# Attention followed by hash-routed experts: a new instruction order in attention, a small slot table for two experts, and the full routing moved behind expert 0

## The chip, the core and the metric

The kernel runs on one core of one Trainium2 chip. A core has TensorE (PE, matrix products), VectorE (DVE) and ScalarE (ACT) for elementwise work, GpSimd (POOL), which also issues the casting and indirect transfers, and SyncE (SP), which issues plain ones. Each engine takes its own instructions in order. The metric is device time in microseconds (us), the median over runs: 375.97 us before the change (3 runs, 375.48 to 377.52).

## The reference

Attention with normed queries and keys over 8 batches, 12 heads, 448 tokens and head size 64; its output, as 3584 rows of 768, goes to one of 8 experts each, chosen by a hash of the token's id.

```python
def rmsnorm(x, g):
    rms = np.sqrt(np.mean(x * x, axis=-1, keepdims=True) + 1e-06)
    return x / rms * g
q_n, k_n = (rmsnorm(q, g_q), rmsnorm(k, g_k))
scores = 1.0 / np.sqrt(64) * np.matmul(q_n, k_n.transpose(0, 1, 3, 2))
scores = scores - np.max(scores, axis=-1, keepdims=True)
attn = np.exp(scores)
attn = attn / (np.sum(attn, axis=-1, keepdims=True) + 1e-09)
x = np.matmul(attn, v)                      # -> (3584, 768)
...
expert_idx = token_ids * np.int64(2654435761) % np.int64(8)
for e in range(8):
    mask = expert_idx == e
    h = np.maximum(x[mask] @ w1[e], 0.0)    # w1[e]: 768 x 1024
    out[mask] = h @ w2[e]                   # w2[e]: 1024 x 768
```

## The kernel before

Attention goes over 48 steps, one for a pair of heads of a batch (6 a batch), in groups of three. For each group, q and k are squared, summed with TensorE, and normed; for each step they are transposed into one PSUM bank (`ps_qk`, one buffer), copied out, multiplied to scores (`ps_sc`, three buffers), put through the exponential on ScalarE, and multiplied with v. The result x goes to a scratch in device memory, batch by batch.

```python
def prep_sq(gi, a, on_act=False):            # a: 1 for k, 0 for q
    ...
    if on_act:
        nc.scalar.activation(dst, f, AF.Square, bias=0.0, scale=1.0)
    else:
        nc.vector.tensor_tensor(out=dst, in0=f, in1=f, op=ALU.mult)
...
def transposes(s, evac=True):
    T32 = ps_qk.tile([P, 512], FP32, name="qkT_ps")
    ...  # 4 transposes of k, 4 of q; then transposed(s): kT and qT copied by VectorE
def score(s, j):
    sc = ps_sc.tile([P, 2, 512], FP32, name="sc_ps")
    ...  # j < 3: two matmuls, then
    nc.scalar.activation(expT[:, 2 * j:2 * j + 2, :], sc[:, :, :S], AF.Exp, bias=0.0, scale=1.0)
    ...  # j == 3: one matmul and one half-size exponential
def av_part(s, part):                        # products with v; part 2 ends with
    nc.vector.reciprocal(srec[:], av[:, :, D])
    nc.vector.tensor_tensor(out=x_sb[...], in0=av[:, :, :D], in1=srec[...], op=ALU.mult)
    if hp == HP - 1:
        store_x(b)
```

The order of one step is written out in a loop, with the routing in small pieces (`side`) between the steps, and the loads of weights at fixed steps:

```python
for s in range(1, NS):
    score(s, 1); score(s, 2)
    if nxt: transposes(s + 1)
    score(s, 3)
    if s == NS - 1:
        for kt in range(KT - 1):             # first rows of expert 0
            put_xT(xg_e[kt], xT_e, kt, bank[:].bitcast(FP16)[:, 0:DIN])
    av_part(s - 1, 0); av_part(s - 1, 1)
    if nxt: score(s + 1, 0)
    ...                                      # pre[s], mid[s], av_part(s - 1, 2), post[s]
    if side and s >= 14:
        side.pop(0)()                        # p1 ... p11, 14 pairs of table(c), table_mm
    if s == NS - 4:
        for kt in range(KT - 1):
            gather(xg_e[kt], gidx[:, kt:kt + 1], N_EARLY)
    if hp == 3:
        if b == 3: w_tiles[0] = [load_w1(0, new_w1(w_pool))]
        if b == 4: w_tiles[0].append(load_w2(0, new_w2(w_pool)))
        if b == 5: w_tiles[1] = [load_w1(1, new_w1(w_pool))]
        if b == 6: w_tiles[1].append(load_w2(1, new_w2(w_pool)))
    if b == 6 and hp == 5:
        w_tiles[2] = w_views(); load_w1(2, w_tiles[2][0])
    if b == 7 and hp == 0:
        load_w2(2, w_tiles[2][1])
```

The routing gives every token a slot: expert times 512 plus its rank there. A matmul over 28 columns of tokens then turns that round into `gidx`, the list of tokens for each slot. Its table lies in one of the two buffers for second-layer weights:

```python
tab = w_pool.tile([P, FO, DIN], FP16, name="w2_sb")[:].rearrange("p a b -> p (a b)")
lo1 = tab[:, 0:NTC * P].rearrange("p (c s) -> p c s", s=P)
hi1 = tab[:, NTC * P:NTC * (P + NHI)].rearrange("p (c s) -> p c s", s=NHI)
...
def table(c):
    V.tensor_scalar(out=lo1[:, c], in0=iota_h[:], scalar1=hl[:, 1, c:c + 1], scalar2=None,
                    op0=ALU.is_equal)
    G.tensor_scalar(out=hi1[:, c], in0=iota_h[:, 0:NHI], scalar1=hl[:, 0, c:c + 1],
                    scalar2=tv[:, c:c + 1], op0=ALU.is_equal, op1=ALU.mult)
```

The experts: rows of x are gathered by token, transposed in TensorE through one PSUM buffer (`turn`), multiplied with w1 (`gemm1`, ReLU shared by ScalarE and VectorE), with w2 (`gemm2`), and scattered to the output.

```python
fetch(1, range(KT - 1)); fetch(0, [KT - 1]); fetch(1, [KT - 1]); fetch(2, range(KT))
queue += w_pieces(3)
for e in range(E):
    if e == 0:
        gemm1(w1_sb, xTs[e], h_sb, 0, EARLY)         # EARLY = 384 of up to 480 rows
        overflow_table()
    else:
        if e + 2 < E: fetch(e + 2, range(KT))
        gemm1(w1_sb, xTs.pop(e), h_sb, 0, FIT)
    w_next(2)
    for kt in range(KT):
        if e == 0 and kt == KT - 1:
            turn(0, kt); gemm1(w1_sb, xTs.pop(0), h_sb, EARLY, FIT); turn(1, kt)
        elif e + 1 < E:
            turn(e + 1, kt)
        gemm2(w2_sb, h_sb, kt, gidx[:, c:c + 1])
        w_next(1)
```

Of the kernel before, what the change touches and what calls it, by code (L numbers as in the profile page):

```python
# [19 lines left out]
def kernel(  # L20
# [45 lines left out]

    SL = 7
# [32 lines left out]
    late = consts.tile([P, 1], FP32)  # L100
    tri = consts.tile([P, EH, NTC], BF16)
# [5 lines left out]
    def setup():  # L107
        import dataclasses as _dc
        tid_t32 = _dc.replace(moe_token_ids.tensor, shape=[N * 2], dtype=I32)
        for base in (0, D):  # L110
            nc.sync.dma_start(out=gcol[base:base + D, 0:1], in_=g_q[:, None])
            nc.sync.dma_start(out=gcol[base:base + D, 1:2], in_=g_k[:, None])
        nc.scalar.dma_start(out=tid32[:],
                            in_=bass.AP(tensor=tid_t32, offset=0,
                                        ap=[[2 * NTC, P], [2, NTC], [1, 2]]))

    def setup2():
# [21 lines left out]
        keep_ge(tri[:], [[NTC, EH], [1, NTC]], -1, -1)  # L139
        G.tensor_copy(iota_f[:], iota_i[:])  # L140
# [35 lines left out]
    gidx = rt_keep.tile([P, NHI], I32)  # L176
    ov_i = rt_keep.tile([P, NOV], I32)


    def gather(xg, idx, rows=N):  # L180
        nc.gpsimd.indirect_dma_start(  # L181
            out=xg[:], out_offset=None, in_=x_dram[0:rows, :],
# [24 lines left out]
    with tc.manual_schedule(), \  # L207
# [66 lines left out]
        def prep_sq(gi, a, on_act=False):  # L274
# [5 lines left out]
            if on_act:  # L280
# [4 lines left out]
        def prep_sum(gi, a, wide=False):  # L285
# [3 lines left out]
            if wide:  # L289
# [17 lines left out]


        def prep_rr(gi):
            n = groups[gi][2]  # L310
            ss = st[gi].pop("ss")
            m = 8 * n
            rr = a_st.tile([P, 2, GMAX * 8, 2], FP16, name="rr")
            nc.scalar.activation(ss[:, :, 0:m], ss[:, :, 0:m], AF.Ln, bias=eps_col[:], scale=1.0 / D)
# [3 lines left out]
            st[gi]["n8"] = a_n8.tile([P, 2, GMAX, 4, 2, D], FP16, name="n8")  # L318

        def prep_norm(gi):  # L320
            n = groups[gi][2]
            rr = st[gi].pop("rr")
            n8 = st[gi]["n8"]
            for a in (1, 0):
                f = raw(a, gi).rearrange("p n (hh j) (u t) -> p n hh j u t", hh=2, t=2)
                for hh in range(2):
                    nc.vector.tensor_tensor(
                        out=n8[:, a, 0:n, :, hh, :].rearrange("p n j (u t) -> p n j u t", t=2),
                        in0=f[:, :, hh],
                        in1=rr[:, a, 4 * n * hh:4 * n * hh + 4 * n].rearrange(  # L330
                            "p (n j) t -> p n j t", j=4)[:, :, :, None, :].to_broadcast(
                                [P, n, 4, D // 2, 2]),
                        op=ALU.mult)
# [9 lines left out]

        rt = lambda shape, dt, name: rt_sb.tile(shape, dt, name=name)
        eid = rt([P, NTC], I32, "eid")
        eidf = rt([P, NTC], FP32, "eidf")
        onehot = rt([P, E, NTC], BF16, "onehot")
        oc = rt([P, E], BF16, "oc")
        cmix = rt([P, 2, P], BF16, "cmix")
        et = rt([P, 2, E], FP32, "et")  # L350
        hole = rt([P, E], FP32, "hole")
        offl = rt([P, E], FP32, "offl")
        t1 = rt([P, E], I32, "t1")
        ot = rt([P, E], FP32, "ot")
        ones_e = rt([P, E], FP32, "ones_e")
        add_e = rt([P, E], FP32, "add_e")
        rank = rt([P, E, NTC], FP32, "rank")
        over = rt([P, E, NTC], FP32, "over")
        slot_f = rt([P, NTC], FP32, "slot_f")
        slot_i = rt([P, NTC], I32, "slot_i")  # L360
        parts = rt([P, 2, NTC], I32, "parts")
        hl = rt([P, 2, NTC], FP32, "hl")
        tab = w_pool.tile([P, FO, DIN], FP16, name="w2_sb")[:].rearrange("p a b -> p (a b)")
# [574 lines left out]
```

## Time and profile before

| | |
|---|---|
| time, median of 3 | 375.97 us |
| span of the profiled run | 374.0 us |
| TensorE busy | 341.5 us, 91% of the span |
| VectorE busy | 213.7 us, 57% |
| ScalarE busy | 189.9 us, 51% |
| GpSimd busy | 174.9 us, 47% |
| mean granted TensorE clock | 0.974 of full speed |
| moved by DMA | 64.59 MB, mean 173 GB/s |

Attention takes the first half of the span and the experts the second, and they have different limits, so the shares over the whole span tell little. The prediction reads the profile by stage. A row of a group gives the source line, the engine and operation, what is written and read with shapes, the count, the busy time and the mean in ns of one. A row of waits gives who waited for whom, the total, the number and the longest wait. A row of the timeline gives start, length, and in brackets the idle time ahead of it with what ended it. In the table by stretches, each engine has its busy time and its instruction count; then come the clock, the mean busy share of the DMA engines as the profile gives it, and GB/s. The digits of the forty slices are tenths of a slice's time.

### The profile page before, as it was taken

The page shows a single profiled execution, that of the slowest core. Times are in us where ns is not written, and L with a number is a line of the kernel's source. Part 1 is how long each engine was busy: PE and PEld are TensorE (multiplying, and loading weights), DVE is VectorE, ACT ScalarE, POOL GpSimd, SP SyncE. Part 2 cuts the span into 40 slices and gives each one's busy share as a digit, 9 for nine tenths or more (in the row PEclk, how much of TensorE's full clock was granted, in tenths as well). Part 3 has the DMA queues.
Part 4 walks back from the last instruction along what each step waited for, and adds up shares of the span by engine and source line. Part 5 has one row for each costly group of instructions (what it writes and reads, how often), then busy time and mean ns, then how long its engine had stood idle before and what let it go on. Part 6 is the DMA issues. An engine that isn't in the chain of part 4 may idle for free. (4 is left out here: it accounts for less than half of the span.)

```text
span 374.0 us, 9220 instructions
## 1 busy us (share of the span) xinstructions
PE 341.5 (91%) x3862; PEld 235.2 (63%) x3862; DVE 213.7 (57%) x514; ACT 189.9 (51%) x288; POOL 174.9 (47%) x246
## 2 busy tenths in 40 slices
PE   7778989999989999998199999999999999999992
PEld 3446656666666666765077676766767676666761
DVE  4577989999999999989033332323232323332311
ACT  5776979999989999999202212111211122121110
POOL 8977981027349920300604855555627445302122
PEclk9998999999999999999669999999999999999998
DMA  8999999928999992299804799999999999702113
GB/s 117 163 184 195 190 221 195 221 35 138 193 212 214 226 198 71 30 207 239 231 10 107 147 279 240 253 246 198 257 195 252 228 189 254 256 23 85 58 42 111
DMA packets 53996, 64.59 MB, mean 173 GB/s; under 512 B 22259, under 2 KB 41990, under 8 KB 53568
## 3 DMA queue, kind: packets, MB, share of 16 engines
q0 software_dynamic: 50320, 57.98, 86.8%
q1 hardware_dynamic: 3024, 5.41, 5.1%
q10 hardware_dynamic: 608, 0.59, 0.6%
q8 instruction: 31, 0.51, 0.6%
q14 instruction: 13, 0.11, 0.1%
HBM read 89.68 MB, written 17.30 MB: 286 GB/s over the span
## 5 line engine op out<-in xcount | busy, mean ns | idle before, releaser
L508 ACT ACTIVATE expT<-sc_ps 128x896 bf16<-128x896 f32 x144 | 125.1, 922 | 10.4 <-PE sc_ps L506 9.2
L790 PEld LDWEIGHTS <-h_sb 128*128 128x128 f16 (+1 forms) x512 | 51.2, 104 | 30.5
L790 PE MATMUL o_ps<-w_sb,h_sb 128*128 128x512 f16 (+3 forms) x384 | 65.8, 326 | 0.0
L795 POOL DMA_INDIRECT out_dram<-o_sb,gidx x32 | 32.5, 1017 | 66.2 <-ACT o_sb L794 36.8
L780 ACT ACTIVATE h_sb<-h_ps 128x480 f16<-128x480 f32 (+2 forms) x36 | 18.8, 526 | 85.9 <-PE h_ps L776 81.2
L776 PEld LDWEIGHTS <-w_sb 128*128 128x128 f16 x336 | 44.3, 146 | 16.6 <-issue 2.2
L181 POOL DMA_INDIRECT xg<-x_scratch,gidx x32 | 32.6, 1019 | 46.1 <-DVE x_sb L551 18.4
L782 DVE TENSOR_SCALAR h_sb<-h_ps 128x480 f16<-128x480 f32 (+2 forms) x36 | 21.7, 602 | 54.9 <-PE h_ps L776 52.1
L776 PE MATMUL h_ps<-xT,w_sb 128*128 128x480 f16 x240 | 49.4, 366 | 0.0
L506 PE MATMUL sc_ps<-qT,kT 64*128 64x448 f16 x288 | 44.6, 360 | 3.7 <-DVE qT L497 1.9
L794 ACT COPY o_sb<-o_ps 128x768 f32<-128x768 f32 x16 | 12.8, 800 | 68.0 <-PE o_ps L790 64.6
L530 PEld LDWEIGHTS <-expT 128*128 128x128 bf16 x864 | 37.8, 99 | 9.5 <-DVE x_sb L551 5.7
L530 PE MATMUL av_ps<-v,expT 128*128 128x65 bf16 x864 | 41.1, 195 | 0.7 <-DVE x_sb L551 0.7
L485 PEld LDWEIGHTS <-n 128*128 128x128 f16 x384 | 22.8, 98 | 24.2 <-issue 14.9
L794 DVE COPY o_sb<-o_ps 128x768 f32<-128x768 f32 (+1 forms) x16 | 15.3, 955 | 38.4 <-PE o_ps L790 27.6
L485 PE MATMUL qkT_ps<-ident,n 128*128 128x128 f16 x384 | 30.7, 222 | 5.8 <-DVE ss L306 2.9
L551 DVE TENSOR_TENSOR x_sb<-av_ps,srec 128x448 f16<-128x448 f32 x48 | 29.7, 619 | 1.5
L193 DVE COPY xT<-xT_ps 128x768 f16<-128x768 f16 x28 | 15.4, 552 | 26.1 <-PE xT_ps L192 26.1
L295 PEld LDWEIGHTS <-ident 128*128 128x128 f16 x544 | 23.5, 98 | 9.0 <-issue 6.3
L513 ACT ACTIVATE expT<-sc_ps 128x448 bf16<-128x448 f32 x48 | 26.8, 558 | 1.1 <-PE sc_ps L511 1.1
L495 DVE TENSOR_SCALAR kT<-qkT_ps,g_col 128x512 f16<-128x512 f16 x48 | 23.0, 480 | 4.9 <-PE qkT_ps L485 4.3
L535 PE MATMUL av_ps<-v,expT 128*128 128x130 bf16 x144 | 25.4, 222 | 0.0
(152 smaller groups left out, 476.8 us busy)
## 6 DMA issues: line engine op xcount, KB each, us to landing
w_sb<-in_moe_w_dram POOLq DMA_DIRECT2D x24, 384.0 KB
w_sb<-in_moe_w_dram POOLq DMA_DIRECT2D x8, 768.0 KB
x_scratch<-x_sb SPq DMA_DIRECT2D x15, 288.0 KB, 7.0
w_sb<-in_moe_w_dram POOLq DMA_DIRECT2D x2, 1536.0 KB
qr<-in_moe_w_dram POOLq DMA_DIRECT2D x8, 384.0 KB
kr<-in_k_dram POOLq DMA_DIRECT2D x6, 384.0 KB
qr<-in_q_dram POOLq DMA_DIRECT2D x3, 768.0 KB
vr<-in_v_dram POOLq DMA_DIRECT2D x6, 384.0 KB
```

The costliest lines, as they stand in the source:

```text
L181: nc.gpsimd.indirect_dma_start(out=xg[:], out_offset=None, in_=x_dram[0:rows, :], in_offset=bass.IndirectOffsetOnAxis(ap=idx, axis=0), bou ...
L485: nc.tensor.transpose(T[:, o:o + P], n8[:, a, i, j].rearrange("p h d -> p (h d)"), ident16[:])
L506: nc.tensor.matmul(sc[:, hh, :S], lhsT=kT[64 * hh:64 * hh + 64, P * j:P * j + P], rhs=qT[64 * hh:64 * hh + 64, :], start=True, stop=True)
L508: nc.scalar.activation(expT[:, 2 * j:2 * j + 2, :], sc[:, :, :S], AF.Exp, bias=0.0, scale=1.0)
L513: nc.scalar.activation(expT[:, 6, :], sc[:, 0, :S], AF.Exp, bias=0.0, scale=1.0)
L530: nc.tensor.matmul(av[:, 2 * t + hh, :], lhsT=expT[:, tl(hh, j), P * t:P * t + P], rhs=v8[:, i, 4 * hh + j, 0:D + 1], start=(hh == 0 and t ...
L535: nc.tensor.matmul(av[:, 2 * t:2 * t + 2, :], lhsT=expT[:, 6, P * t:P * t + P], rhs=v8[:, i, 3::4, 0:D + 1], start=False, stop=False)
L551: nc.vector.tensor_tensor(out=x_sb[:, :, hp * D:hp * D + D], in0=av[:, :, :D], in1=srec[:, :, None].to_broadcast([P, SL, D]), op=ALU.mult)
L776: nc.tensor.matmul(h_ps[:, :c1 - c0], lhsT=w1v[:, co, fo, :], rhs=xT[:, co, c0:c1], start=(co == 0), stop=(co == CO - 1))
L790: nc.tensor.matmul(o_ps[0:w, d0:d1], lhsT=h_sb[:, fo, col * P:col * P + w], rhs=w2_sb[:, fo, d0:d1], start=(fo == 0), stop=(fo == FO - 1))
L794: (nc.vector.tensor_copy if col % 2 else nc.scalar.copy)(o_sb[0:w], o_ps[0:w])
L795: scat = nc.gpsimd.indirect_dma_start(out=out[:, :], out_offset=bass.IndirectOffsetOnAxis(ap=idx[0:w], axis=0), in_=o_sb[0:w], in_offset=N ...
```

## The change

It has four parts.

1. The order of attention's instructions is no longer a loop body with hooks but a list of tokens, found by a search: a long list for the first ten steps and one of a group's length (`steady`) for all later groups. The operations are the same. Warm-up matmuls (`spin`) stand in the list so that TensorE doesn't stand idle at the start. The square of k of groups 0 and 3 goes to ScalarE (before: k of groups 1 and 2, q of group 1).
2. In attention only a small table is made, with slots of 32 by 15, for experts 0 and 1 alone; it is all that the first gathers need. It works on few wide VectorE operations and needs nothing of GpSimd.
3. The full routing (p2 to p11, the 28 columns of the table, its matmul) is put into expert 0's work and early expert 1's, on VectorE and TensorE only; ReLU of expert 0 goes to ScalarE alone.
4. Loads are spread: smaller pieces of q, k and v at the start and earlier later on, weights at other steps, w2 of expert 2 after attention. The full table no longer lies in a weight buffer. Gathers of the last tile of an expert fetch 96 rows instead of 128.

```diff
-        def prep_sq(gi, a, on_act=False):
+        ACT_SQ = ((0, 1), (3, 1))
+        WIDE_SUM = ((0, 0), (1, 0), (1, 1))
+        def prep_sq(gi, a):
...
-        tab = w_pool.tile([P, FO, DIN], FP16, name="w2_sb")[:].rearrange("p a b -> p (a b)")
...
+        def m7():
+            V.tensor_tensor(out=hi[:], in0=hv[:, None, :].to_broadcast([P, NTC, 2 * HI0]),
+                            in1=wide(parts_h[:, 0], 2 * HI0), op=ALU.is_equal)
+        def m8():
+            V.tensor_tensor(out=hi[:], in0=hi[:], in1=wide(tv16, 2 * HI0), op=ALU.mult)
+        def m9():
+            V.tensor_tensor(out=lo[:], in0=iota_h[:, None, 0:LO0].to_broadcast([P, NTC, LO0]),
+                            in1=wide(parts_h[:, 1], LO0), op=ALU.is_equal)
...
+        side = [m1, m2, m3, m4, m5, m6, m7, m8, m9, m10]
+        SIDE0, SIDEN = 13, 2
+        def hooks(s):
...
+            if s == HP:
+                load(4, 0, HP)
+            if hp == 3 and 1 <= b and b + 4 < B:
+                load(b + 4, 0, HP)
+            if side and s >= SIDE0 and (s - SIDE0) % SIDEN == 0:
                 side.pop(0)()
             if s == NS - 4:
                 for kt in range(KT - 1):
                     gather(xg_e[kt], gidx[:, kt:kt + 1], N_EARLY)
+            if s == 24:
+                w_tiles[0] = [load_w1(0, new_w1(w_pool))]
+            if s == 27:
+                w_tiles[0].append(load_w2(0, new_w2(w_pool)))
+            if s == 30:
+                w_tiles[1] = [load_w1(1, new_w1(w_pool))]
+            if s == 33:
+                w_tiles[1].append(load_w2(1, new_w2(w_pool)))
+            if s == 37:
                 w_tiles[2] = w_views()
                 load_w1(2, w_tiles[2][0])
-            if b == 7 and hp == 0:
-                load_w2(2, w_tiles[2][1])
...
+        emit("""
+            zero:2 zero:5 zero:0 sqk:0 zero:1 sqq:0 spin:9 sumq:0 zero:4 redq:0 zero:3 spin:4
+            sumk:0 redk:0 ln:0 sqq:1 gain:0 er:0 nk:0.0 nk:0.1 spin:4 sumq:1 sqk:1 nq:0.0 spin:1
...
+        """, 0, 0)
+        steady = """
+            Tk:1 Tq:1 sc:0.1 sc:0.2 av:-1.0 kT:1 av:-1.1 qT:1 exp:0.1 exp:0.2 v:1 sc:0.3 sumq:1
+            sqk:2 redq:1 av:-1.2 sc:1.0 sc:1.1 exp:0.3 ln:1 sc:1.2 er:1 Tk:2 exp:1.0 Tq:2 rec:-1
+            x:-1 av:0.0 nk:1.0 kT:2 qT:2 av:0.1 exp:1.1 sc:1.3 av:0.2 sumk:2 sc:2.0 exp:1.2
+            nk:1.1 sc:2.1 exp:1.3 nq:1.0 sc:2.2 exp:2.0 rec:0 nq:1.1 redk:2 Tk:3 x:0 Tq:3 av:1.0
+            kT:3 exp:2.1 av:1.1 qT:3 sqq:2 sc:2.3 av:1.2 rec:1 sc:3.0 exp:2.2 exp:2.3 x:1 exp:3.0
+        """
+        for g in range(4, NG):
+            emit(steady, g, s0[g])
...
+        def table(c):
+            V.tensor_scalar(out=lo1[:, c], in0=iota_h[:], scalar1=hl[:, 1, c:c + 1], scalar2=None,
+                            op0=ALU.is_equal)
+            V.tensor_scalar(out=hi1[:, c], in0=iota_h[:, HB:NHI], scalar1=hl[:, 0, c:c + 1],
+                            scalar2=tv[:, c:c + 1], op0=ALU.is_equal, op1=ALU.mult)
...
+        pairs = [(lambda c=c: (table(c), table(c + 1))) for c in range(0, NTC, 2)]
+        plan = {
+            (0, "g", 0): [p2], (0, "g", 2): [p3], (0, "g", 3): [p4, p5], (0, "g", 5): [p6],
+            (0, "g", 6): [p7, p8], (0, "g", 7): [p9, p10],
+            (0, "k", 0): [p11] + pairs[0:3], (0, "k", 1): pairs[3:8], (0, "k", 2): pairs[8:13],
+            (0, "k", 3): pairs[13:], (1, "g", 2): [table_mm, lambda: fetch(2, range(KT)),
+                                                   lambda: fetch(3, range(KT))],
+            (1, "k", 0): [overflow_table],
+        }
+        blank(10)
         fetch(1, range(KT - 1))
         fetch(0, [KT - 1])
         fetch(1, [KT - 1])
-        fetch(2, range(KT))
+        load_w2(2, w_tiles[2][1])
         queue += w_pieces(3)
...
             if e == 0:
-                gemm1(w1_sb, xTs[e], h_sb, 0, EARLY)
-                overflow_table()
+                gemm1(w1_sb, xTs[e], h_sb, 0, EARLY, False, after)
```

In a token, the letters name the operation and the first number the step or group, counted from the current one: `Tk`, `Tq` transposes, `kT`, `qT` their copies, `sc` and `exp` scores and exponentials by quarter, `av` products with v, `rec` and `x` the last scaling, `sqk`, `sumk`, `redk`, `ln`, `er`, `nk` the norm. In `plan`, "g" stands for a column block of the first layer and "k" for a tile of the second.

## The prediction

> **What bounds the kernel now.** I read the page's forty slices first, because this program has stages with different limits.
>
> ```profile
> PE   7778989999989999998199999999999999999992
> PEclk9998999999999999999669999999999999999998
> DMA  8999999928999992299804799999999999702113
> ```
>
> Each slice is 9.35 us. TensorE has a hole in slice 20 (178 to 187 us) and a lowered clock in slices 20 and 21; ahead of it lies attention, behind it the experts. The second view cuts the span at the events that I found in the timeline: first exponential (13.4), a steady stretch of 36 head pairs between two stores of x (45.1 to 166), last exponential (179.8), first second-layer matmul of expert 0 (202.1 with its transposes), first matmul of expert 1 (218.1).
>
> ```profile
> core 0: us, PE busy (x) PEld busy (x) DVE busy (x) ACT busy (x) POOL busy (x), PEclk, DMA share, GB/s
> 13.40:45.10 31.70, 26.25 (x396) 17.25 (x392) 23.96 (x55) 25.59 (x39) 25.45 (x42) 0.95 1.53 186
> 45.10:166.00 120.90, 114.62 (x2007) 80.73 (x2003) 115.56 (x300) 112.49 (x169) 52.61 (x86) 1.00 1.06 166
> 166.00:179.80 13.80, 10.97 (x172) 6.68 (x169) 11.19 (x31) 13.48 (x19) 1.41 (x2) 1.00 1.09 226
> 179.80:202.10 22.30, 14.69 (x125) 11.97 (x126) 5.00 (x10) 1.88 (x5) 5.77 (x6) 0.69 0.41 114
> 202.10:218.10 16.00, 15.25 (x144) 11.15 (x143) 5.98 (x14) 2.60 (x6) 11.50 (x13) 1.00 0.72 158
> 218.10:374.00 155.90, 149.04 (x930) 101.78 (x928) 45.00 (x67) 27.18 (x42) 65.92 (x74) 0.99 0.79 184
> ```
>
> Four readings. The ramp (first row) has ScalarE at 25.59 of 31.7 us. In the steady stretch VectorE (96%) and ScalarE (93%) are both nearly full, so neither alone is the bound: small waits move between them. From 179.8 to 202.1 the vector engines are idle and the TensorE clock is 0.69. From 218 on, TensorE runs through; the page has it at 9 in every slice up to the last one, and the change leaves that stage alone. The end of the chain of waits is only the last scatter, so it says nothing here.
>
> Why the hole? The waits and the timeline around it:
>
> ```profile
> POOL w_sb L167 <- PE sc_ps L506: 22.7, 1, 22.7
> PE qkT_ps L192 <- DMA xg<-x_scratch,gidx: 7.3, 1, 7.3
> ```
> ```profile
> 156.68 2.45 POOL L162 DMA_DIRECT2D qr<-in_moe_w_dram  x4
> 159.09 0.61 POOL L167 DMA_DIRECT2D kr<-in_moe_w_dram  x1
> ...
> 178.09 1.14 POOL L181 DMA_INDIRECT xg<-x_scratch,gidx  x1 [18.39 <-DVE x_sb L551]
> ```
>
> The second-layer weights of expert 1 share their buffer with the routing table (`tab`), so GpSimd, which issues in order, stands for 22.7 us until the table has been used up (156.06). Then three 1,536 KB loads go out at once: w2 of expert 1, w1 and w2 of expert 2. In that stretch the DMA answer for 150 to 192 us gives the stores of x (issued 166.0 to 168.4) 8.2 and 9.1 us to landing, against 2.5 at the least over the whole run. The first gather can go only at 178.09, and its rows arrive at 185.46. TensorE idles 7.3 us, and then runs at half clock until about 194. The seam between the two halves costs both.
>
> **What the skill says.** "TensorE: Matmul & The Clock Gate", Part 1 (the HAM clock gate), says that an idle window of some 3.4 us puts TensorE back to half clock and that as long a busy stretch restores it. The trace agrees as to the fall: 0.50 from 182 to 190 after the idle 7.3 us; the return took longer than the page says, to about 194. "DMA: Bandwidth & Descriptors", SWDGE vs HWDGE vs iDMA, says there is one software queue, and that an engine goes round between queues: gathers line up behind weights, SP stores share with them. The 8.2 us and the 7.4 us from gather to data fit. "Perfetto Trace Analysis", Identifying the Most-Contended Engine, counts occupancy as fair for VectorE and ScalarE but not for TensorE; so I take the 114.62 us of TensorE in the steady stretch as no bound. "VectorE: DVE Perf Modes", The TRN2 errata, gives (N+151)/0.96 ns for an fp32 tensor_tensor; the 224-element row here takes 379 ns against 391 by that formula.
>
> **The change part by part.**
>
> (1) Routing out of attention. Removed from VectorE there: 28 table operations of 254 ns (7.1 us), eight 224-element ones of about 0.38 to 0.57 (3.2 us), some fifteen small ones of about 0.2 (3 us): 13.3 us.
>
> ```profile
> L452 DVE TENSOR_SCALAR w_sb<-iota_h,hl 128x128 f16<-128x128 f16 x28 | 5.9, 254 | 0.0
> ```
>
> (The row's 5.9 us of busy time leaves overlap with neighbours out, so 12 us is safer than 13.) Added: three wide comparisons of 840 or 896 elements with a broadcast operand, an estimate by the formula above of 1.05 us each (3.2), and 23 small ones of 0.2 (4.6): 7.8 us. Net −4 to −5.5 us, so VectorE falls from 115.6 to about 111 in the steady stretch and ScalarE's 112.5 becomes the largest. All table work leaves GpSimd (28 x 743 ns).
>
> (2) New order. It takes no work away from ScalarE; it can only close idle. If ScalarE reaches 96.5% in the steady stretch, it lasts 112.5/0.965 = 116.6 us, −4.3. In the ramp the square of k goes to ScalarE while VectorE squares q, norms are interleaved, and zero fills are split; at 92% instead of 81% the ramp lasts 25.6/0.92 = 27.8, −3.9. The first exponential may come 0.5 us earlier. The end stretch is full already (13.48 of 13.8). The last exponential thus ends near 171.1 instead of 179.8: −8.7.
>
> (3) Loads spread. The table no longer sits in the weight buffer; w2 of expert 1 is issued at pair 33, w1 of expert 2 at pair 37, w2 of expert 2 after attention. By the 3.36 us a pair that the steady stretch shows, pair 37 lies some 30 us ahead of the last exponential, and 1,536 KB at the 187 to 270 GB/s of that stretch are 6 to 8 us. So DMA is empty when x of batch 6 is stored, 13 us ahead of the last exponential. A store without company landed in about 4 us (the ACT-issued one, 4.1); gathers then start some 8 us ahead and are there about when the last score is through. From the last exponential T: the three rounds of transposes (0.50) and copies (0.56), about 1.25 each, begin 1.9 ahead of T as the last score does now (177.8), and end at T+1.9; the last attention products 1.6; 48 matmuls at 4.06/24 = 0.17 us are 8.1; together T+11.6, and with the routing's few matmuls T+12. Now it is 202.4−179.8 = T+22.6. Gain 10.6 us.
>
> (4) Full routing behind expert 0. The second-layer stage of expert 0 lasts 16.0 us, and VectorE now has 5.98 us in it. It loses 1.0 (ReLU goes to ScalarE) and 1.0 (overflow table), and gains 28 pairs of table operations, 0.22 + 0.20 = 0.42 each (the second by the small rows of about 0.2): 11.8, and 0.7 ahead of them. That is 16.4 us of work in 16.0, in strict order with copies that wait for TensorE. Walking it by tile: the table operations placed after tile 1 (ten pairs, 4 us) begin only after that tile's 0.96 us output copy, so the copy of the third transposed tile comes late, and the single buffer of transposes then holds TensorE. I get about 2 us there and 2 more behind the next ten pairs: +4. The 28 table matmuls moved into expert 1 lie bare on TensorE: 28 at some 40 ns, +1.2. Rows of expert 2 are fetched then; by the 1.3 us from one gather to the next they have about 5 us of slack, if the weights of expert 3 have drained: 0.
>
> Sum: −8.7 −10.6 +4.0 +1.2 = −14.1 us. 375.97 − 14.1 = 361.9, rounded to **362 us**.
>
> **Rivals.** First, VectorE becomes the bound behind expert 0: the late copies cost 7 to 9 us instead of 4, and the fetch of expert 2 comes late too, another 2 or 3. For it: 16.4 us of work in order in 16.0, one buffer for transposes. Against: the operations are small, and a stall is made up for by later slack. Time then: about 368 to 370. Second, the searched order misses on the chip: each pair still loses a wait at the single bank of transposes, so attention gains nothing. For it: it was fixed ahead of time, and three engines over 93% leave little to gain. Against: ScalarE's idle in the steady stretch comes as 9.2 us of waits for scores, just what an order can cure, and the VectorE load falls anyway. Time then: about 370. Third, the hole closes but the gathers still come late by 2 to 3 us because GpSimd is 1.3 us a gather and the store takes its 6.6 us median: 364. Fourth, the good way: ScalarE at 98.5% in the steady stretch and 95% in the ramp, no stall behind expert 0: 353 to 354.
>
> **Range and chances.** The hole is worth 10 us with little doubt; attention between 0 and 12; the stage behind expert 0 between 0 and −10. Both ends together are unlikely, so 353 to 371 should hold it 8 times in 10. Two per cent is 7.5 us, that is 368.5; to miss it, both the first and second rival would have to come in part. Faster 0.81, same 0.14, slower 0.05.
>
> **What would show it.** Right: no TensorE wait for a gather above 2 us at the seam, no 6 in the clock row, first gather issued some 8 us ahead of the last exponential, that exponential near 171, ScalarE at 96% in the steady stretch, waits of TensorE for VectorE copies of about 4 us behind expert 0. Wrong: a gather wait or half clock at the seam (then step 3), a distance of the stores of x still near 20.15 us (then step 2), more than 28 us from the first second-layer matmul to expert 1's first (then step 4), or a wait for rows of expert 2.

## The result, and the profile after

The changed kernel takes 365.8 us in the median of 4 runs (364.5 to 366.3), the kernel before beside it 375.9 (375.5 to 377.5). The ratio is 0.9718, with a 95% interval of 0.9679 to 0.9757. The prediction said 362, within 353 to 371. This first pair turned out not to be the whole story: the same kernel was run in two more sets, and in one of them nearly all of the gain was gone (375.9 against 377.4), as the third part of the experiments shows.

The forty slices of the changed kernel, to be read against those of before:

```profile
PE   7887999999998999998793999999999999999992
...
PEclk9999999999999999999998799999999999999998
DMA  8999989999999999833459986999999999602112
```

The hole of TensorE in the middle, with its 6 in the clock row, is gone. A smaller one is new behind it (the slices with clock 8 and 7, 191 to 209 us). The table by stretches, cut at the same events as before: first exponential, first store of x, seventh store of x, end of the last exponential, first transposes of expert 0's second-layer stage, expert 1's first matmul:

```profile
core 0: us, PE busy (x) PEld busy (x) DVE busy (x) ACT busy (x) POOL busy (x), PEclk, DMA share, GB/s
13.22:43.76 30.54, 24.34 (x402) 16.43 (x399) 24.36 (x57) 25.35 (x38) 28.54 (x55) 1.00 1.26 152
43.76:158.64 114.88, 110.57 (x1989) 78.86 (x1987) 109.16 (x276) 109.39 (x168) 47.77 (x78) 1.00 1.20 198
158.64:172.77 14.13, 12.38 (x208) 8.13 (x206) 11.38 (x30) 14.13 (x20) 5.59 (x6) 1.00 0.44 110
172.77:185.03 12.26, 10.39 (x101) 8.85 (x99) 8.26 (x33) 3.33 (x8) 2.08 (x3) 1.00 0.35 91
185.03:207.18 22.15, 16.27 (x145) 12.18 (x142) 14.18 (x63) 4.10 (x11) 7.48 (x10) 0.85 1.00 216
207.18:363.90 156.72, 149.81 (x958) 102.53 (x956) 47.52 (x78) 27.19 (x42) 69.71 (x78) 0.99 0.75 179
```

Stage by stage against before (in us): the first store of x comes at 43.76 instead of 45.11 (−1.35); the steady stretch lasts 114.88 instead of 120.92 (−6.0); the last exponential ends at 172.77 instead of 179.82 (−7.05 in all). From there to the second-layer stage of expert 0 it is 12.26 instead of 22.24 (−10.0). That stage takes 22.15 instead of 16.03 (+6.1). Expert 1's first layer, up to its first second-layer matmul, takes 10.82 instead of 10.06 (+0.8). From there on both kernels need the same time, 145.9 and 145.8. The sum is −10.1; the profiled spans, 363.9 and 374.0, differ by just that.

The waits of TensorE in the changed kernel between 185 and 218 us show where the 6.1 comes from (who waited for whom: total, times, longest):

```profile
PE h_ps L764 <- DVE xT_e L212: 3.6, 1, 3.6
PE xT_ps L211 <- DVE xT L212: 2.2, 1, 2.2
```

TensorE waits twice for a copy of transposed rows on VectorE. The groups of the changed kernel show what VectorE does meanwhile, 28 table operations of each kind, and the table's matmuls:

```profile
L940 DVE TENSOR_SCALAR hi<-iota_h,hl,tv 128x56 f16<-128x56 f16 x28 | 8.4, 311 | 0.0
L938 DVE TENSOR_SCALAR lo<-iota_h,hl 128x128 f16<-128x128 f16 x28 | 7.2, 257 | 0.0
L946 PE MATMUL h_ps<-hi,lo 128*128 128x56 f16 x28 | 0.9, 187 | 0.0
```

Started one after the other, a pair takes 0.37 us. VectorE's timeline has ten pairs ahead of the copy that the first wait ends with, and ten more ahead of the copy that the second ends with:

```profile
191.11 0.96 DVE L784 COPY o_sb<-o_ps 128x768 f32<-128x768 f32 x1 [1.53 <-PE o_ps L780]
191.98 0.24 DVE L938 TENSOR_SCALAR lo<-iota_h,hl 128x128 f16<-128x128 f16 x1
...
195.44 0.29 DVE L940 TENSOR_SCALAR hi<-iota_h,hl,tv 128x56 f16<-128x56 f16 x1
195.64 0.55 DVE L212 COPY xT<-xT_ps 128x768 f16<-128x768 f16 x1
...
199.57 0.29 DVE L940 TENSOR_SCALAR hi<-iota_h,hl,tv 128x56 f16<-128x56 f16 x1
199.78 0.55 DVE L212 COPY xT_e<-xT_ps 128x768 f16<-128x768 f16 x1
```

The third thing to see is GpSimd's own timeline in the changed kernel:

```profile
117.13 0.59 POOL L185 DMA_DIRECT2D w_sb<-in_moe_w_dram  x1 [1.18 <-DMA w_sb<-in_moe_w_dram]
...
132.90 0.61 POOL L180 DMA_DIRECT2D qr<-in_moe_w_dram  x1 [1.83 <-DMA w_sb<-in_moe_w_dram]
...
165.65 1.12 POOL L200 DMA_INDIRECT xg<-x_scratch,gidx  x1 [32.13 <-DVE qT L483]
```

All weights for attention's end are out by 133 us, then GpSimd stands ready for 32 us, and the first gather goes at 165.65, 7.1 us ahead of the last exponential.

### The profile page after: what moved, and what is told of

It is laid out like the page before. It is cut to its first block, busy times and chain, and to the rows that moved or that the text cites. A ratio compares the mean times of both kernels' runs of the same rounds, so it can differ in the third digit from the quotient of the medians.

```text
span 363.9 us, 9341 instructions
## 1 busy us (share of the span) xinstructions
PE 333.8 (92%) x3882; PEld 232.1 (64%) x3882; DVE 223.2 (61%) x573; ACT 188.4 (52%) x293; POOL 173.2 (48%) x252
## 5 line engine op out<-in xcount | busy, mean ns | idle before, releaser
L509 ACT ACTIVATE expT<-sc_ps 128x896 bf16<-128x896 f32 x144 | 123.1, 941 | 5.5 <-PE sc_ps L491 5.3
L768 ACT ACTIVATE h_sb<-h_ps 128x480 f16<-128x480 f32 (+2 forms) x44 | 21.8, 498 | 80.8 <-PE h_ps L764 74.3
L770 DVE TENSOR_SCALAR h_sb<-h_ps 128x480 f16<-128x480 f32 x28 | 18.4, 658 | 45.1 <-PE h_ps L764 45.1
L491 PE MATMUL sc_ps<-qT,kT 64*128 64x448 f16 x288 | 41.9, 354 | 3.4 <-DVE qT L483 1.6
L526 PEld LDWEIGHTS <-expT 128*128 128x128 bf16 x864 | 36.1, 97 | 8.7 <-DVE x_sb L555 7.6
L267 POOL DMA_DIRECT2D kr<-in_k_dram x40 | 25.7, 655 | 13.3 <-DMA qr<-in_q_dram 8.7
L317 PEld LDWEIGHTS <-ident 128*128 128x128 f16 x544 | 24.5, 98 | 9.0 <-issue 4.3
L267 POOL DMA_DIRECT2D vr<-in_v_dram x40 | 26.4, 679 | 4.4 <-DMA kr<-in_k_dram 3.3
L512 ACT ACTIVATE expT<-sc_ps 128x448 bf16<-128x448 f32 x48 | 28.1, 585 | 0.6 <-PE sc_ps L494 0.6
```

The costliest lines, as they stand in the source:

```text
L267: eng.dma_start(out=dst[64 * half:64 * half + 64, :, s0:s0 + cnt, :].rearrange("p n s d -> p n (s d)"), in_=runs(t, h0 + hh, 2, n, tok0, s ...
L491: nc.tensor.matmul(sc[:, hh, :S], lhsT=kT[64 * hh:64 * hh + 64, P * j:P * j + P], rhs=qT[64 * hh:64 * hh + 64, :], start=True, stop=True)
L512: nc.scalar.activation(expT[:, 6, :], sc[:, 0, :S], AF.Exp, bias=0.0, scale=1.0)
L526: nc.tensor.matmul(av[:, 2 * t + hh, :], lhsT=expT[:, tl(hh, j), P * t:P * t + P], rhs=v8[:, i, 4 * hh + j, 0:D + 1], start=(hh == 0 and t ...
```

## The experiments

The runs came in sets. All kernels of one set, and the kernel before with them, ran on one chip. Sets 2 to 5 were on four different chips; the chip of set 1 is not on record. Most kernels ran 18 to 20 times; "after", c1, e5, e7, e9 and e10 ran four times, so a difference of 0.5% between two of these means little. This table has the stages of every profiled run. "Pairs" is the time from the second to the seventh store of x, 30 head pairs; "end" from the seventh store to the end of the last exponential T; "seam" from T to expert 0's second-layer stage; "stage" the length of that; "next" from expert 1's first matmul to its first second-layer matmul. All but the ratio are in us.

| run | set | time | ratio to before, 95% | pairs | end | seam | stage | next |
|---|---|---|---|---|---|---|---|---|
| before | 1 | 375.9 | 1 | 100.46 | 13.79 | 22.24 | 16.03 | 10.06 |
| after | 1 | 365.8 | 0.968 to 0.976 | 97.51 | 14.13 | 12.26 | 22.15 | 10.82 |
| e1 old order | 2 | 376.3 | 0.997 to 1.001 | 99.44 | 19.06 | 14.83 | 22.34 | 11.78 |
| e2 buffer held | 2 | 377.9 | 1.002 to 1.007 | 97.61 | 14.13 | 22.36 | 21.82 | 10.85 |
| e3 table moved | 2 | 374.3 | 0.990 to 0.994 | 100.35 | 18.21 | 15.19 | 15.89 | 10.06 |
| e4 ScalarE copies | 2 | 374.8 | 0.995 to 0.999 | 97.66 | 19.41 | 15.19 | 16.46 | 15.40 |
| c1 after | 3 | 366.4 | 0.971 to 0.982 | 97.67 | 14.13 | 12.26 | 21.87 | 11.52 |
| e5 k early | 3 | 366.9 | 0.971 to 0.983 | 97.40 | 14.14 | 12.26 | 22.04 | 12.37 |
| e6 filler | 3 | 373.5 | 0.991 to 0.996 | 104.77 | 14.13 | 12.26 | 21.90 | 11.32 |
| e7 w2 back | 3 | 366.5 | 0.968 to 0.981 | 97.50 | 14.13 | 12.26 | 22.37 | 10.82 |
| c2 after | 4 | 375.9 | 0.996 to 1.000 | 97.69 | 18.50 | 13.49 | 21.89 | 11.00 |
| e8 table moved | 4 | 375.5 | 0.992 to 0.996 | 100.32 | 19.13 | 14.47 | 16.41 | 10.06 |
| e9 rows early | 4 | 370.0 | 0.972 to 0.985 | 97.86 | 19.44 | 14.95 | 17.16 | 11.18 |
| e10 shifted | 5 | 368.6 | 0.972 to 0.982 | 97.40 | 18.99 | 15.67 | 17.16 | 10.50 |

### What the steady stretch gained from: order or VectorE's load

e1 gives the changed kernel the old order from the fifth group on:

```diff
-            Tk:1 Tq:1 sc:0.1 sc:0.2 av:-1.0 kT:1 av:-1.1 qT:1 exp:0.1 exp:0.2 v:1 ...
+            sc:0.1 exp:0.1 sc:0.2 exp:0.2 Tk:1 Tq:1 kT:1 qT:1 sc:0.3 exp:0.3 av:-1.0 ...
```

> The changed kernel with the old instruction order for the groups of the steady stretch; ramp, loads and routing stay as changed. Theory (the order carries most of the 6.0 us that the steady stretch gained): 3 to 6 us more than the changed kernel's 365.8, so 369 to 372, and the distance of the stores of x grows to 118 to 121 us over the steady stretch, although VectorE keeps its lighter load of about 109 us there. Rival (the lighter VectorE load of 109 instead of 115.6 us carries it, whatever the order): 0 to 1.5 us more, 366 to 367.5, and the steady stretch stays near 115.

e6 leaves the new order and adds the table work that the change took from VectorE, on top of the small table:

```diff
+            if 14 <= s < 22:
+                V.tensor_tensor(out=dwb[:], in0=dwa[:], in1=dwa[:], op=ALU.add)
+            if 22 <= s < 36:
+                for _ in range(2):
+                    V.tensor_scalar(out=dum[:], in0=iota_h[:], scalar1=late[:], scalar2=None,
+                                    op0=ALU.is_equal)
```

> The changed kernel with VectorE's old load put back into attention as filler whose results nobody reads: eight additions of 224 fp32 elements and 28 comparisons of 128x128. Theory (new order absorbs it): the steady stretch grows by 0 to 2 us over 114.9. Rival (VectorE's load is what the steady stretch hangs on): it grows by 3 to 6 us, to 118 to 121.

The 30 pairs in the table by stretches, of the changed kernel run again (c1), of e6 and of e1:

```profile
60.86:158.53 97.67, 93.36 (x1675) 66.29 (x1673) 92.48 (x236) 92.39 (x141) 33.26 (x51) 1.00 1.23 208
```
```profile
60.60:165.37 104.77, 94.65 (x1675) 66.16 (x1673) 100.40 (x273) 93.07 (x141) 32.92 (x51) 1.00 1.14 193
```
```profile
61.11:160.55 99.44, 94.56 (x1674) 67.49 (x1671) 95.12 (x235) 93.53 (x141) 33.03 (x50) 1.00 1.18 201
```

The total of e1 says nothing, since its seam was disturbed (below); the pairs are not touched by that. From the first to the seventh store e1 takes 117.77 us, short of the 118 to 121 expected, against 120.92 before and 114.88 after. So of the 6.0 us gained, 3.1 came without the new order of the steady stretch, with VectorE's lighter load and the rest of the change, and 2.9 with it. Both theories were half right. In the 30 pairs alone it is 1.0 without and 1.9 with the order (100.46, 99.44, 97.51). Most of the 3.1 lies between the first two stores of x, and there the lighter load is not the only candidate: in the kernel before VectorE waits 1.5 us for v from a load, and neither e1 nor the changed kernel has this wait. How the 3.1 is shared between load and earlier transfers is not shown. e6 shows how the new order depends on VectorE: 7.9 us more of VectorE work (100.40 against 92.48) cost 7.1 us, 0.9 for each. This is more than the old load, since VectorE had 97.31 us of work in these pairs before. At the same 0.9, the new order with 97.31 us would take some 102 us against 100.46 with the old order; this is an estimate from e6 and c1. By it the new order leaves little slack on VectorE and pays because the table went out. A limit: the filler stands closer together than the routing did before.

### The seam: what made the hole, and what cleared it

e2 holds the second weight buffer until pair 39, as the routing table did, and loads w2 of expert 2 inside attention:

```diff
+        hold = w_pool.tile([P, FO, DIN], FP16, name="w2_sb")[:, 0, 0:8]
...
+            if s == 39:
+                V.tensor_copy(held[:], hold)
...
+            if s == 42:
+                load_w2(2, w_tiles[2][1])
```

> The changed kernel with the second weight buffer held until pair 39, as the routing table held it before, and the load of w2 of expert 2 back in attention; order and routing stay as changed. Theory (the shared buffer holds GpSimd, three loads of 1,536 KB then go out in one burst and stand before the stores of x and the gathers): the wait of TensorE for gathered rows and the half clock return at the seam, first second-layer matmul 18 to 22 us after the last exponential instead of 12.3, 374 to 378 in all. Rival (the smaller table and the order of the end of attention closed the hole by themselves): no wait for rows above 2 us, 365 to 368.

The waits of e2 between 120 and 195 us:

```profile
POOL w_sb L185 <- DVE held L677: 33.4, 1, 33.4
...
PE qkT_ps L211 <- DMA xg<-x_scratch,gidx: 8.1, 1, 8.1
```

Everything of before comes back: GpSimd stands 33.4 us, three loads of 1,536 KB go at 150.5 to 154.1, the first gather at 171.47, TensorE waits 8.1 us for its rows, and the seam is 22.36 us, against 22.24 before. The loads delay the stores of x, and the gathers must wait for these. The seventh batch's stores, with the time from issue to landing in us, first in e2, then in the changed kernel:

```profile
x_scratch<-x_sb SPq DMA_DIRECT2D x2, 288.0 KB, 7.8
x_scratch<-x_sb SPq DMA_DIRECT2D x2, 48.0 KB, 9.1
```
```profile
x_scratch<-x_sb SPq DMA_DIRECT2D x2, 288.0 KB, 3.6
x_scratch<-x_sb SPq DMA_DIRECT2D x2, 48.0 KB, 3.8
```

The first gather goes 12.1 us after the first of these stores in e2, and 7.0 after it in the changed kernel. e7 takes away the hold but keeps w2 of expert 2 inside attention:

```diff
+            if s == 42:
+                load_w2(2, w_tiles[2][1])
...
-        load_w2(2, w_tiles[2][1])
```

> The changed kernel with w2 of expert 2 loaded inside attention again, at its old place in the program, with no buffer held. Theory (GpSimd runs ahead and the load has drained long before the last store of x): the gathers go out as early as in the changed kernel, within 1 us of its time. Rival (moving this load out is part of what cleared the seam): 2 to 6 us more, and a wait of TensorE for gathered rows above 2 us.

Seam 12.26, time 366.5 beside c1's 366.4. So that part of the change did nothing here; GpSimd had issued the load at 135.7, long ahead. With e7, only the hold is left as the cause of what e2 shows: the theory is shown.

The inverse, e3 and again e8, is the kernel before with nothing changed but the place of the table:

```diff
-        tab = w_pool.tile([P, FO, DIN], FP16, name="w2_sb")[:].rearrange("p a b -> p (a b)")
-        lo1 = tab[:, 0:NTC * P].rearrange("p (c s) -> p c s", s=P)
-        hi1 = tab[:, NTC * P:NTC * (P + NHI)].rearrange("p (c s) -> p c s", s=NHI)
+        lo_x = xT_e[:].rearrange("p c t -> p (c t)").rearrange("p (c s) -> p c s", s=P)
+        lo_r = rt([P, 4, P], FP16, "lo_r")
+        hi1 = rt([P, NTC, NHI], FP16, "hi_r")
```

> The kernel before with one thing changed: the full routing table lies in other memory than the weight buffer. Order, routing and loads' places in the program stay as before. Theory (the sharing alone made the hole): the hole goes, the first second-layer matmul comes 12 to 14 us after the last exponential instead of 22.3, 365 to 368 in all, which is the whole net gain of the change. Rival (the load of w2 of expert 2 inside attention or the large table is needed for the hole too): 373 to 376.

> The kernel before with the full routing table moved out of the weight buffer, a second time. Theory (sharing alone made the hole, and the stall of the first trial belongs to the chip): first second-layer matmul 12 to 13 us after the last exponential, last exponential near 180, 365 to 367. Rival (gathers that go out while the last scores are computed disturb attention in this kernel by themselves): 372 to 375 again, last exponential near 185.

The wait for gathered rows went, and the seam fell to 15.19 and 14.47 us. But the last exponential came at 184.96 and 187.16, not near 180, since the "end" stretch grew from 13.79 to 18.21 and 19.13. In e8, 2.5 us more were lost between the first two stores. Net, a gain of 0.8 and 0.6%. The theories' times are missed. e3 falls into its rival's range, but not for the rival's reason, since the wait for rows did go; e8's rival, that gathers disturb attention, is nearly what came (375.5, last exponential at 187.2). What ate the gain is the next part. This kernel was never run on a chip without the disturbance, so what the place of the table alone is worth there stays open.

### A stop of TensorE while the gathers move

In e1, e3 and e4 the end stretch was 4 to 5 us longer than in the recorded pair, although nothing had been changed there in e4. So the changed kernel itself was run again, twice, in other sets.

> The changed kernel once more, unchanged, beside the others. In three of the first four experiments TensorE's semaphore updates came 2 to 4 us late while the gathers moved (171 to 177 us), and the clock fell to half behind it; the first profile of the changed kernel shows none of this. If the stall hangs on where the instructions of the variants lie, this run is free of it: 365 to 367, last exponential near 172.8. If it hangs on the chip or on chance, it shows it too: 372 to 376, last exponential at 177 to 180.

> The changed kernel unchanged, beside the two that follow. The stall of 2 to 4 us at the seam was there in three variants timed together, and in none of the four kernels timed together after them. If it belongs to the chip that a set of runs falls on, this run and the two beside it all show it (last exponential 177 to 180 here, 372 to 376) or none does (172.8, 365 to 367). If it belongs to the variants, this run is free of it and the repeat of the kernel with the moved table shows it.

The same kernel, TensorE's timeline in c1 and then in c2, in the stretch where the gathers move:

```profile
168.74 0.32 PE L538 MATMUL av_ps<-v,expT 128*64 128x65 bf16 x8
168.99 1.22 PE L491 MATMUL sc_ps<-qT,kT 64*128 64x448 f16 x6
170.25 0.54 PE L526 MATMUL av_ps<-v,expT 128*128 128x65 bf16 x12
```
```profile
170.41 0.32 PE L538 MATMUL av_ps<-v,expT 128*64 128x65 bf16 x8
170.66 0.79 PE L491 MATMUL sc_ps<-qT,kT 64*128 64x448 f16 x4
173.54 0.56 PE L491 MATMUL sc_ps<-qT,kT 64*128 64x448 f16 x2 [2.09 <-issue]
176.25 0.84 PE L526 MATMUL av_ps<-v,expT 128*128 128x65 bf16 x12 [2.15 <-DVE xg L970]
```

In c1 the six score matmuls and what follows run through; in c2 TensorE stops for 2.1 us after four of them and for 2.2 after the last two. The second wait is put down to VectorE, but VectorE was itself waiting: its own timeline in c2 has it idle for TensorE all that while.

```profile
175.10 0.20 DVE L545 RECIPROCAL srec<-av_ps 128x7 f32<-128x7 f32 x1 [4.71 <-PE sc_ps L491]
```

The reciprocal needs the product of 170.41, whose record ends at 170.73, and starts at 175.10. So TensorE's results, or its signals, came more than 4 us late. "Perfetto Trace Analysis", Summary: the profiler window per engine type, says that a TensorE record ends at an estimated end, and so which of the two it was can't be read here. The clock is at 0.50 from 172.98 to 179.80: the last matmuls above take 0.84 us for what took 0.54. The kernel pays with 4.4 us in the end stretch and 1.2 in the seam. (The two profiled spans differ by 8.1. Of the rest, 1.7 lies ahead of the second store of x and is taken up at the end; 1.3 lies behind the start of expert 1's second layer, and 0.5 is won back just ahead of it. The profiled execution of c2 was the fastest of its 20, 373.8 us; between the medians of c2 and c1 there are 9.5 us, of which the profiles leave 1.4 unexplained.) The gathers themselves look alike: 384 packets in both, 23% of the DMA engines' time from 160 to 178 us.

The stop goes with the set: it is in every kernel of sets 2, 4 and 5 whose gathers move under attention, and in none of the five profiles of the changed kernel and its variants in sets 1 and 3. Within set 2 it needs the gathers: e2, whose first gather goes out only 2.0 us ahead of its last exponential and whose rows arrive after it, has an end stretch of 14.13 us, to the hundredth that of the undisturbed runs, beside 19.06, 18.21 and 19.41. The kernel before takes 375.9 to 377.4 us in all five sets; its gathers go out 1.7 us ahead of its last exponential (set 1), as late as those of e2. With the stop the changed kernel is worth 0.2% (c2, the only such run of it as it stands), without it 2.4 and 2.8%. Each of the four known chips was used in one set only, so a property of the chip and one of the occasion can't be told apart; where this text says chip, it means this.

One cause was tried. In c2, e1, e4 and e9 a packet of 16 KB moved on the instruction queue right at the stop, and the theory was that TensorE waits for its own next instructions. e10 moves all of TensorE's later instructions on by 120, in a kernel that is otherwise e9:

```diff
-            for _ in range(cnt):
-                nc.tensor.matmul(wps[:, 0:448], lhsT=warm[:, 0:P], rhs=warm[:, 0:448],
+            n, w = (4 * cnt, 112) if cnt >= 3 else (cnt, 448)
+            for _ in range(n):
+                nc.tensor.matmul(wps[:, 0:w], lhsT=warm[:, 0:P], rhs=warm[:, 0:w],
```

> The kernel of the ninth experiment with 120 more TensorE instructions in the idle start (60 of the warming matmuls cut into four narrow ones each; the same columns), so that every later TensorE instruction stands 120 places further on. Where the seam stalled, TensorE stopped with its 5,304th to 5,308th record, at which a packet of 16 KB moved on the instruction queue, while the gathers were moving; in the sets without the stall that packet moved at the same record and nothing stopped. Theory (TensorE waits for its next instructions, fetched behind the gathers): the packet now moves at about the old record 5,185, ahead of the gathers, and the next at about 5,440, behind them, so no stop at the seam on any chip: last exponential near 173, 360 to 361. Rival (the gathers hold TensorE whatever it fetches): on a chip that stalls it stops again, at another record, 368 to 370 as in the ninth experiment. On a chip that doesn't stall both give 360 to 361, and the question stays open.

TensorE's timeline in e10:

```profile
171.67 0.55 PE L491 MATMUL sc_ps<-qT,kT 64*128 64x448 f16 x4 [1.23 <-DVE qT L483]
175.15 0.37 PE L491 MATMUL sc_ps<-qT,kT 64*128 64x448 f16 x2 [2.92 <-ACT expT L512]
```

It stops at the same matmuls, while the packet had moved at 166.53, ahead of the first gathered data at 167.7. The theory falls. e8 says the same: its packets moved at 169.21 and 181.98, and TensorE stood for 2.0 us up to 180.96, between them. What in the gathers holds TensorE, and why in some sets only, stays open.

### The stage behind expert 0

e4 puts all copies of that stage on ScalarE and leaves VectorE the tables:

```diff
-            (nc.vector.tensor_copy if col % 2 else nc.scalar.copy)(o_sb[0:w], o_ps[0:w])
+            (nc.vector.tensor_copy if col % 2 and not act else nc.scalar.copy)(o_sb[0:w], o_ps[0:w])
...
-            put_xT(xgs.pop(e * KT + kt), xTs[e], kt, bank[:])
+            put_xT(xgs.pop(e * KT + kt), xTs[e], kt, bank[:], copy)
```

> The changed kernel with all copies of expert 0's second-layer stage (transposed rows and outputs) on ScalarE, so that VectorE does the routing tables alone there. Theory (table operations in VectorE's strict order delay the copies): the two waits of TensorE of 2.24 and 3.64 us vanish, and with them the half clock of the 48 matmuls behind them (4.00 instead of 3.04 us): 359 to 361 in all. Rival (the one bank of transposes, or ScalarE's own slower copies, hold TensorE anyway): 364 to 366. Second rival (the tables come later or take as long, and the first layer of expert 1 waits for the rows of expert 2): 366 to 369.

The stage in e4's table by stretches, and the longest wait of TensorE behind it:

```profile
193.99:210.45 16.46, 15.21 (x145) 11.28 (x143) 11.63 (x61) 8.48 (x17) 7.48 (x10) 1.00 0.96 193
```
```profile
PE xT_ps L211 <- DMA xg<-x_scratch,gidx: 4.4, 1, 4.4
```

The stage falls from 22.15 to 16.46 us at full clock: the theory is right for the stage. The time isn't, first because of the stop, and then because the wait moved: TensorE now needs the rows of expert 2 earlier, while their gathers still go out inside expert 1's first layer, at 216.36, though the last table operation had ended at 205.8. e9 keeps e4's copies and moves the table's matmuls and the gathers up:

```diff
-            (0, "k", 3): pairs[13:], (1, "g", 2): [table_mm, lambda: fetch(2, range(KT)),
-                                                   lambda: fetch(3, range(KT))],
+            (0, "k", 3): pairs[13:] + [table_mm, lambda: fetch(2, range(KT)),
+                                       lambda: fetch(3, range(KT))],
```

> The changed kernel with expert 0's copies on ScalarE as in the fourth experiment, and with the table's matmuls and the gathers of experts 2 and 3 put right behind the last table operation, ahead of expert 1's first layer instead of inside it. In the fourth experiment the stage of expert 0 fell from 22.1 to 16.5 us, but TensorE then waited 4.4 us for the rows of expert 2, whose gathers went out at the same place as before although the table was ready 8 us earlier. Theory: both waits are gone, 5.5 us less than the changed kernel beside it, 360 to 361 where that one has 366. Rival (the gathers wait behind the weights of expert 3 in the queue wherever they are issued): 364 to 366.

TensorE's timeline in e9, from the table's matmuls on:

```profile
210.55 0.89 PE L946 MATMUL h_ps<-hi,lo 128*128 128x56 f16 x28
211.28 9.92 PE L764 MATMUL h_ps<-xT,w_sb 128*128 128x480 f16 x48
222.11 0.51 PE L211 MATMUL xT_ps<-ident,xg 128*128 128x128 f16 x6 [0.91 <-PE h_ps L764]
```

Both waits are gone but for 0.9 us. Beside the changed kernel on the same chip e9 is 5.9 us faster (369.95 against 375.89), about the 5.5 expected, although it had the stop too. (In the two profiles the stage and "next" together are 4.6 us shorter; c2's profile was its fastest execution.) The absolute 360 to 361 was missed. It beats both kernels of this study there. On a chip without the stop it wasn't run; by the difference it would take some 360, which is an estimate.

### The ramp

After the recorded pair, VectorE's wait of 2.6 us for the k of batch 1's second half looked like what the ramp hangs on. e5 loads that k earlier:

```diff
-        load(1, 0, 3, "kqv")
+        load(1, 0, 3, "kq")
+        load(1, 3, 3, "k")
+        load(1, 0, 3, "v")
+        load(1, 3, 3, "qv")
```

> The changed kernel with the k of the second half of batch 1 loaded ahead of the first half's v. Theory (the ramp's 2.61 us wait of VectorE for that k holds the whole pipeline): 2 to 2.5 us less than the changed kernel beside it, and the first store of x comes 2 us earlier after the first exponential. Rival (another wait takes its place, since v comes later): 0 to 0.5 us less.

The rival is nearer: the first store of x came at 42.96 instead of 43.40 (c1), and the time is the same within its spread, 366.9 against 366.4. c1 itself had only 0.5 us of that wait and its store came just 0.4 us earlier than in the recorded pair, so the edit had little left to win there. What holds the ramp stays open. What e5 gained it lost at once, through the overlap told at the end.

## Why the prediction was right, and where it was not

The time is within the range, 3.8 us above the prediction of 362, and the parts hold as follows.

**Step 1, routing out of attention.** VectorE was to fall to about 111 us in the steady stretch; it fell to 109.16. "ScalarE's 112.5 becomes the largest" was too simple: they are level (109.39), and by e6 the stretch still follows VectorE's load nearly one to one.

**Step 2, new order.** In the steady stretch the sum was under-sized, −6.0 instead of −4.3, and the term itself over-sized: by e1 only 2.9 belong to the order. The sign named for it, ScalarE at 96%, was nearly met (109.39 of 114.88, 95%), but ScalarE's busy time fell by 3.1 us as well (1.6 of it in the 30 pairs), where the prediction held it at 112.5. The prediction also misread a view: the "9.2 us of waits for scores" are those from 13.4 to 179.8; in the steady stretch they are 5.4. In the ramp the term failed: "at 92% instead of 81% the ramp lasts 27.8, −3.9" became 30.54 in the recorded pair, 25.35 of it ScalarE, so 83% (29.11 in c1, 87%). With the first exponential's −0.5, the first store of x was to come 4.4 us earlier and came 1.35 earlier. In sum the last exponential gained 7.05 instead of 8.7.

**Step 3, loads spread.** The first second-layer matmul comes at T+12.6 against T+12 predicted (its transposes at T+12.26, the seam of the table), and e2 shows the cause. The signs came: no wait for a gather at the seam, first gather 7.1 us ahead of T. The way to it was wrong in one point. "w2 of expert 1 is issued at pair 33, w1 of expert 2 at pair 37" reads the program's pair numbers as times; GpSimd runs ahead of the others, and the loads went at 117 and at 119 to 133 us, while pairs 30 to 34 were in their exponentials; pair 37 came at 140. And moving w2 of expert 2 was no part of the gain (e7).

**Step 4, full routing behind expert 0.** +4.0 was mis-sized; it measured +6.1. The two stalls were there, at the copies foreseen, with 2.24 and 3.64 us instead of 2 and 2, although a pair of table operations takes 0.37 us and not 0.42. So most of the miss is the second stall, where nearly all of ten pairs lies bare. A missing term is the clock: it is 1.00 over the first wait and 0.60 over the second, and the 48 narrow matmuls behind take 4.00 us instead of 3.04. (The three make 6.84; the stage before had 0.75 us of small waits of its own, which are gone.) "TensorE: Matmul & The Clock Gate", Part 1, has half clock after an idle window of some 3.4 us. These traces fit only roughly: the clock falls at 197.49, 0.75 us into the second wait and 3.5 us after the first began, with 0.5 us of transposes between them. In the kernel before, it fell at 180.30, 2.1 us after TensorE's wait began, so the prediction's "agrees as to the fall" was too kind as well. In e4, waits of up to 1.3 us leave the clock at 1.00 through the stage. The table's matmuls took 0.89 us; expert 1's first layer grew by 0.8 instead of 1.2. No row of expert 2 was late in the recorded pair; in c1 and e5 TensorE waited 0.5 and 1.4 us for them, so the slack was thinner than the 5 us predicted.

**The rivals.** The first (copies cost 7 to 9 and rows come late) was half of it: 6.1, no late rows. The second, third and fourth didn't happen in the recorded pair. None of the rivals named what the experiments found: that TensorE can stop while gathers move under attention, and that with it nearly all of the 10 us was gone in c2: 5.6 us by the profiles through the stop and the seam, the rest in smaller parts. On that chip the predicted 362 would have been wrong by 14 us, outside its range. That it was right rests on the chip the pair ran on.

## What to carry to other kernels

When an in-order queue stands for a buffer, look at what goes out in a burst behind it: the cost of the shared buffer here was not GpSimd's idle time but the stores and gathers behind three large loads, and keeping the buffer free was worth 10 us where nothing else stood in the way. When work is moved off a full engine, move its consumers' place in the program too, and check the copies that stand in line with it: e9 took 5.9 us by doing both. A gain of 3% that depends on transfers moving under busy engines should be measured on more than one chip.

## What the runs showed that I had not expected

The stop at the seam is the first. The second goes with the stretch between the first two stores of x, which takes 17.4 us in some runs of the changed order and 18.8 in others, with the same work. Set the timeline of the changed kernel in the first set against c2, copies of v on VectorE and zero fills on GpSimd:

```profile
46.59 2.08 POOL L644 MEMSET xg<- 128x768 f16 x3
...
49.57 0.55 DVE L358 COPY v<-vr 128x1536 bf16<-128x1536 bf16 x1
```
```profile
49.02 2.08 POOL L644 MEMSET xg<- 128x768 f16 x3
...
49.52 2.00 DVE L358 COPY v<-vr 128x1536 bf16<-128x1536 bf16 x1
```

Where GpSimd's fill lies under it, the copy takes 2.00 us instead of 0.55, and ends 0.4 us behind the fill. The same pair of rows is in e2, e4, e7, e9 and e10 (1.99 or 2.00, stretches of 18.8), and in e5 the copy takes 2.63 (19.4), which is where its earlier k went; c1 and e6 have 0.55 and 17.5 and 17.4. No run changed this overlap alone. "GPSIMD Engine Reference", 1. Specifications, says that the two engines share their access to SBUF and that VectorE's two-port modes collide with it; these rows agree as to the collision, and do not show which mode the copy ran in. Whether the two overlap is worth 1.4 us of this stretch; how much of it reaches the end of the kernel is not shown.
